# Gated linear attention with an MLP-mixer behind it, one core: u of batch 0 built transposed in PSUM, weight pieces of three chunks, another order

## The chip, the core and the metric

One core of one Trainium2 chip runs the whole program. The metric is the device time of one execution in microseconds; the time of a kernel is the median of its runs.

## The reference, cut to what matters

```python
# attention: q, k, v, alpha are (4 batches, 8 heads, 768 steps, 48)
for t in range(S):
    state = alpha[:, :, t, :, None] * state + einsum('bhd,bhe->bhde', k[:, :, t], v[:, :, t])
    y[:, :, t] = einsum('bhd,bhde->bhe', q[:, :, t], state)
# x is y with its heads side by side: (4, 768, 384)
# token and channel mixer, w_tok1 (768, 256), w_tok2 (256, 768), w_ch1 (384, 1536), w_ch2 (1536, 384)
h = maximum(x.T @ w_tok1, 0) @ w_tok2
u = x + h.T
out = u + maximum(u @ w_ch1, 0) @ w_ch2
```

Inputs and output are float32.

## The kernel before

The work of a batch is attention in three chunks of 256 time steps (chunks n = 0 to 11 over the four batches, `NB = 3`) and then a mixer. Every operation is written down once in `build` as `P.op(name, engines, ...)`, and two tables of numbers and names, `ORDER` and `BUFS`, say on which engine and in which place of that engine's program each stands, and which buffer it uses. A name in `ORDER` carries its engine as last letter: t is TensorE (PE), s ScalarE (ACT), v VectorE (DVE), g GpSimd (POOL), y the queue of SyncE (SP), which starts the loads, some stores and the transposing DMAs. Each engine takes its list strictly in that order and waits at an operation until what it reads is there.

Of a chunk n: `ld_at`, `ld_kt`, `ld_qt`, `ld_vt` load alpha, k, q and v (384 KB each). ACT takes the logarithm (`ln`), PE sums it over time (`cum`), ACT makes the decays `E` and `IE`, and `kk`, `qq` scale k and q (line 700). They are turned by PE (`trk`, `trq`, line 712, chunks 0 to 5) or by a transposing DMA (`dk`, `dq`, chunks 6 to 11), and `evk`, `evq`, `pq` copy them out. PE forms the masked scores (`G0`, `G1`; DVE masks them in line 770), the sums for the state (`K`), what comes from the state (`ia`, `ib`) and the outputs (`y0`, `y1`). The state runs on through `sa` (DVE, line 841) and `sm` (POOL or DVE, line 844): `sm1` of a chunk feeds the next. `vb`, `vs`, `ka`, `kb`, `kc` are casts and copies that bring v and k to other partitions. `P`, `k0a`, `q0r` are elementwise products. `x0`, `x1` evict the chunk's output as one of the six x tiles of a batch.

Of a batch b: `t1_b_m_kc` (line 878) multiplies with the first token weight, `ht` applies relu, `t2_b_i` (line 883) multiplies with the second one and gives the i-th 128 rows of h; `u_b_i` (DVE, line 887) adds x. The first channel product needs u transposed. For batch 0 (`UP = (0,)`) PE does that with 18 identity products of 128 columns (`up_0_p`, line 894) and three copies bring them from PSUM to `ut`; for batches 1 to 3 a transposing DMA on SP's queue does it (`ux_b_half`). `c1_b_mc_half` (line 902, three matmuls) and its relu `rt`, `c2_b_i_q4` (line 907, three matmuls), the sum `o` with u (DVE, line 911) and the store `st` end the batch. `f..` are fillers: PE multiplies zeros into an unused bank where it would else stand still.

The weights come as 16 pieces of 384 KB (`ldw_`), each cast to bf16 (`cw_`, line 746) by POOL, ACT or DVE. A piece of w_ch1 holds one chunk of 128 rows by 768 columns, so that each `c1` with mc below 6 needs pieces 0, 1 and 2, and the others need 3, 4 and 5:

```python
preds=(uts[0:2 + half] if b in UP else [uts[half]]) + [wl[("wc1", p)] for p in ((0, 1, 2) if mc < 6 else (3, 4, 5))]
```

Both pieces of w_tok2 (128 of its 256 rows each) are needed by every `t2`.

Of the kernel before, what the change touches and what calls it, by code (L numbers as in the profile page):

```python
# [56 lines left out]
def either(*ds):  # L57
    out = {}
    for d in ds:
        out.update(d)  # L60
    return out
# [40 lines left out]
UP = (0,)  # L102
# [18 lines left out]
def build(g):  # L121

    P = Plan()
# [6 lines left out]
    def fillers():  # L130
        for o in list(P.ops):
            nm = o.name
            if "PE" in o.eng and (nm[:4] in ("t1_0", "t2_0", "up_0") or nm.split("_")[-1][-1] in "0123" and nm[:2] not in ("t1", "t2", "up", "c1", "c2") and not nm.endswith("10") and not nm.endswith("11")):
# [182 lines left out]
    def mixer(b):  # L316
# [15 lines left out]
        us = []  # L332
        for i in range(NS):
            if i % 3 == 0:
                u = V("u")
            bank = V("one")
            o = P.op(f"t2_{b}_{i}", pe([384] * 2), m0 + (1900 + 330 * i) * sc, writes=[bank],
                     reads=[h for h, _ in hts], preds=[h for _, h in hts] + [wl[("wt2", p)] for p in range(2)],
                     emit=lambda e, i=i, bank=bank: g.tok2(bank, i, [h for h, _ in hts]))
            uo = P.op(f"u_{b}_{i}", dve(384), m0 + (1950 + 330 * i) * sc, writes=[u], reads=[bank, x[i][0]], preds=[o],  # L340
                      emit=lambda e, i=i, bank=bank, u=u: g.uadd(u, i, bank, x[i][0]))
            us.append((u, uo))
        ut = V("ut")
        uts = []
        if b in UP:
            for p in range(3):
                bank = V("one")
                o = P.op(f"up_{b}_{p}", pe([128] * 6), m0 + (3900 + 340 * p) * sc, writes=[bank],
                         reads=list(dict.fromkeys([us[2 * p][0], us[2 * p + 1][0]])),
                         preds=[us[2 * p][1], us[2 * p + 1][1]],  # L350
                         emit=lambda e, p=p, bank=bank: g.utr(bank, [us[2 * p][0], us[2 * p + 1][0]], p))
                uts.append(P.op(f"ut_{b}_{p}", either(dve(768, True), act(768)), m0 + (3950 + 340 * p) * sc, writes=[ut],
                                reads=[bank], preds=[o], emit=lambda e, p=p, bank=bank: g.utev(e, ut, bank, p)))
        else:
            for half in range(2):
                uts.append(P.op(f"ux_{b}_{half}", {"SP": (1240.0, 1240.0)}, m0 + (3900 + 500 * half) * sc, writes=[ut],
                                reads=[us[3 * half][0]], preds=[us[3 * half + i][1] for i in range(3)],
                                emit=lambda e, half=half: g.uxbar(ut, us[3 * half][0], half),
                                dma=("x", 1450.0, 1180.0, 480.0)))
# [13 lines left out]
        for i in range(NS):  # L373
            hold = 4000.0 if (i >= NS - 3 and b < B - 1) else 0.0
            cuts = [(0, HD // 2), (HD // 2, HD)] if (b, i) == LAST else [(0, HD)]
            for ci, (ca, cz) in enumerate(cuts):
# [33 lines left out]
ld_at1y ld_at0y ln1s ln0s f8_cumw1t f1_cumw1t cumw1t IE1s cumw0t IE0s ld_vt0y E0s vb0g vs0_0g vs1_0v ld_kt0y kk0v  # L410
f8_trk0t f1_trk0t trk0t E1s ld_qt0y qq0v ka0s kb0s kc0v f1_trq0t trq0t ld_kt1y kk1v K0t evq0s s0_0v ld_vt1y vb1s
f1_trk1t trk1t ld_at2y evk0v ln2s f2_G0_0t G0_0t ld_qt1y ka1g sa1_0v f4_cumw2t cumw2t mask0_0v vs0_1s kb1g kc1g vs1_1s
K1t sm1_0g qq1v sa0_1v sm0_1v G1_0t ld_kt2y IE2s E2s trq1t evq1s ib0t mask1_0v f3_y1_0t y1_0t y0_0t evk1v G0_1t sa1_1v
ld_qt2y x1_0s mask0_1v G1_1t ld_vt2y x0_0s vb2s kk2g trk2t kc2s ldw_wt10y qq2g cw_wt10s f2_ia1t ia1t mask1_1v evk2s
trq2t ld_at3y vs1_2g ldw_wt11y evq2v ib1t y1_1t y0_1t vs0_2g ldw_wt21y sm1_1g P3g K2t sa0_2v sm0_2g x0_1s t1_0_0_0t
f1_G0_2t G0_2t ldw_wt20y G1_2t cw_wt20g t1_0_1_0t mask0_2v x1_1s t1_0_1_1t ld_at4y ld_kt3y t1_0_1_2t lnP3s cum3t
cw_wt11s IE3s ia2t y0_2t x0_2s t1_0_0_1t t1_0_0_2t E3s t1_0_0_3t mask1_2v t1_0_1_3t ib2t y1_2t ldw_wc14y t1_0_1_4t
x1_2s t1_0_0_4t f1_t1_0_1_5t t1_0_1_5t ht_0_1v P4g cw_wt21s t1_0_0_5t ht_0_0s f3_t2_0_0t t2_0_0t t2_0_1t u_0_0v ln13s
r13s ldw_wc13y t2_0_2t u_0_1v t2_0_3t u_0_2v t2_0_5t lnP4s t2_0_4t u_0_3v u_0_5v u_0_4v up_0_0t cw_wc14s cw_wc13s
ldw_wc15y up_0_1t ld_qt3y k0a3g kk3g cum4t trk3t cw_wc15g ut_0_0v up_0_2t ut_0_2v ut_0_1s c1_0_11_0t c1_0_8_0t IE4s  # L420
c1_0_11_1t rt_0_8_0v rt_0_11_0v ldw_wc11y q0r3g qq3g c1_0_9_1t rt_0_9_1v ln14s kb3s c1_0_10_0t cw_wc11s c1_0_9_0t
rt_0_9_0v rt_0_11_1v E4s c1_0_7_0t c1_0_10_1t c1_0_7_1t ldw_wc10y r14s cw_wc10s rt_0_10_1v trq3t evk3s rt_0_7_0v
ldw_wc12y ld_vt3y cw_wc12g c1_0_2_0t c1_0_0_1t ka3g rt_0_7_1s c1_0_8_1t rt_0_10_0v vb3v vs1_3g vs0_3g rt_0_0_1v
rt_0_2_0v evq3s ld_at5y ld_qt4y c1_0_1_1t rt_0_8_1v c1_0_3_0t kc3s K3t P5g c1_0_4_1t rt_0_3_0s rt_0_1_1s q0r4g G0_3t
ld_kt4y qq4g s0_3v ln15s G1_3t sa1_3v c1_0_2_1t rt_0_2_1s mask0_3v lnP5s c1_0_1_0t c1_0_5_1t rt_0_5_1s rt_0_1_0s r15s
mask1_3v ldw_wc21y cw_wc21s k0a4g ldw_wc20y c1_0_6_1t rt_0_6_1v c1_0_4_0t kk4v ldw_wc22y c1_0_5_0t c1_0_0_0t cw_wc22s
rt_0_4_0v rt_0_0_0v cw_wc20g rt_0_4_1s c1_0_6_0t rt_0_6_0v c1_0_3_1t trq4t rt_0_3_1v cum5t trk4t ld_kt5y k0a5g
ldw_wc23y rt_0_5_0s c2_0_3_0t c2_0_5_0t evq4s kb4s evk4v ld_qt5y G1_4t mask1_4v G0_4t ld_vt4y c2_0_0_0t IE5s c2_0_0_1t
ka4g cw_wc23s c2_0_3_1t kc4s sm1_3g E5s mask0_4v ib3t y1_3t ldw_wc24y cw_wc24s c2_0_5_1t vb4g vs1_4s x1_3s ia4t
ldw_wc25y vs0_4g cw_wc25s ld_at6y y0_3t kk5v c2_0_3_2t y0_4t q0r5v trk5t evk5s qq5v K4t c2_0_0_2t sa0_4v c2_0_0_3t P6v  # L430
x0_3s ld_at7y sm0_4g o_0_0v trq5t x0_4s sa1_4v P7g evq5s lnP6s c2_0_5_2t c2_0_5_3t ld_vt5y vb5g c2_0_4_0t c2_0_4_1t
ld_kt7y kc5g G1_5t G0_5t lnP7s o_0_5v ib4t y1_4t vs1_5s mask1_5v t1_1_1_0t t1_1_1_1t sm1_4g x1_4s c2_0_4_2t c2_0_3_3t
vs0_5s ld_at8y t1_1_1_2t st_0_5s K5t mask0_5v sa0_5v sm0_5v cum6t t1_1_0_0t ld_kt6y k0a6g t1_1_0_1t ld_qt6y c2_0_2_0t
ln17s ld_qt7y ia5t y0_5t x0_5s IE6s kk6g ib5t y1_5t ln16s E6s t1_1_0_2t x1_5v t1_1_0_3t t1_1_1_3t cum7t E7s o_0_3v
t1_1_1_4t t1_1_1_5t r16s ld_kt8y q0r6g ld_vt6y dk6y P8g ht_1_1v lnP8s t1_1_0_4t t1_1_0_5t c2_0_2_1t c2_0_2_2t ln18s
ht_1_0v t2_1_1t u_1_1v t2_1_2t t2_1_0t t2_1_4t u_1_2v u_1_0v ux_1_0y c2_0_1_0t c2_0_1_1t vb6s IE7s qq6v r17s t2_1_3t
u_1_3v c2_0_2_3t ka6s kc6s t2_1_5t o_0_2v u_1_4v c2_0_1_2t st_0_0y st_0_3s cum8t k0a8g c2_0_1_3t u_1_5v q0r7v vs1_6v
dq6y c2_0_4_3t c1_1_8_0t rt_1_8_0v IE8s c1_1_11_0t vs0_6s c1_1_5_0t E8s c1_1_10_0t o_0_4v c1_1_4_0t k0a7g ux_1_1y
o_0_1v kb6g rt_1_4_0v pq6s K6t s0_6v sa1_6v c1_1_3_0t rt_1_3_0v c1_1_0_0t rt_1_5_0s ld_at9y rt_1_0_0v rt_1_11_0s
# [526 lines left out]
```

## Time and profile before

| | us |
|---|---|
| time, median of 3 runs | 163.17 (162.33 to 164.11) |
| span of the profiled execution, first to last instruction | 160.5 |
| PE busy | 154.6 (96%) |
| DVE, ACT, POOL busy | 114.9, 97.8, 80.8 |
| mean DMA rate | 218 GB/s |

The profiled execution has no time beside its span; the table's first row comes from other executions, which also count what lies before the first and behind the last instruction. Rows of the profile give start and duration in us from the span's start. "PE" rows are matmuls, whose duration (some 326 ns for 384 columns) runs through the pipeline, so that matmuls overlap: the pace is the time from one start to the next. "PEld" rows are the weight loads beside them.

### The profile page before, as it was taken

How to read it: one execution, taken by the hardware profiler on the slowest of the kernel's cores; microseconds unless marked ns; L12 is line 12 of the kernel's file. 1: busy time of each engine (PE TensorE's matmuls, PEld its weight loads, DVE VectorE, ACT ScalarE, POOL GpSimd, SP SyncE). 2: the span in 40 equal slices, each digit the busy share in tenths (PEclk: the TensorE clock that was granted, in tenths of full speed). 3: DMA queues.
4: the chain of work that ended last, by engine and by line, in shares of the span. 5: the costliest groups of instructions: out<-in, count | busy, mean ns of one | idle time of the engine just before them, and what ended most of it. 6: DMA issues, size and time to landing. Idle time of an engine off the chain costs nothing.

```text
span 160.5 us, 3971 instructions
## 1 busy us (share of the span) xinstructions
PE 154.6 (96%) x1563; PEld 97.1 (60%) x1563; DVE 114.9 (72%) x206; ACT 97.8 (61%) x179; POOL 80.8 (50%) x94
## 2 busy tenths in 40 slices
PE   7999989999999999999999999999999999999992
PEld 2545565766667676666667666566567665665661
DVE  6099994979889787989969758795886762464222
ACT  3789999998899955897563583269832203343000
POOL 5205897695973649389778852699523000000000
PEclk9999999999999999999999999999999999999999
DMA  4999999999999999999989999989701235111133
GB/s 122 320 324 317 317 374 311 339 333 306 316 347 324 275 278 272 210 228 319 241 202 298 239 315 204 217 196 134 196 21 62 87 79 169 49 49 53 49 129 116
DMA packets 76130, 35.05 MB, mean 218 GB/s; under 512 B 70352, under 2 KB 74320, under 8 KB 76112
## 3 DMA queue, kind: packets, MB, share of 16 engines
q1 hardware_dynamic: 73808, 31.76, 74.1%
q10 hardware_dynamic: 2304, 3.05, 5.3%
q8 instruction: 12, 0.20, 0.5%
q14 instruction: 6, 0.05, 0.1%
HBM read 25.17 MB, written 4.72 MB: 186 GB/s over the span
## 4 chain that ended last, share of the span: by engine, by line
PE 61%; DMA 12%; DVE 6%; ACT 6%; SPq 6%; POOL 4%; issue 3%; DVEq 0%; POOLq 0%
PE ps L907 22%; PE ps L902 21%; PE ps L643 11%; DMA in<-in_v_dram 6%; SPq L584 6%; DMA out_dram<-o 4%; PE ps L878 3%; PE ps L883 2%; DMA ut<-u 2%; DVE pkk L700 2%; DVE gtm L770 1%; PE ps L712 1%; DVE rt L875 1%; POOL vb L746 1%; POOL pkq L700 1%
## 5 line engine op out<-in xcount | busy, mean ns | idle before, releaser
L907 PE MATMUL ps<-wc,rt 128*128 128x384 bf16 (+1 forms) x300 | 52.4, 319 | 0.0
L902 PE MATMUL ps<-ut,wc 128*128 128x384 bf16 x288 | 50.3, 326 | 0.1
L902 PEld LDWEIGHTS <-wc 128*128 128x128 bf16 x288 | 27.1, 98 | 17.9 <-DMA ut<-u 0.6
L907 PEld LDWEIGHTS <-rt 128*128 128x128 bf16 x300 | 27.8, 98 | 16.0
L873 ACT ACTIVATE rt<-ps 128x384 bf16<-128x384 f32 x47 | 21.4, 492 | 23.6 <-PE ps L902 23.3
L875 DVE TENSOR_SCALAR rt<-ps 128x384 bf16<-128x384 f32 x49 | 25.6, 551 | 9.1 <-PE ps L902 8.9
L770 DVE TENSOR_TENSOR gtm<-ps,mk 128x1024 bf16<-128x1024 f32 x24 | 28.5, 1218 | 3.1 <-PE ps L643 2.8
L911 DVE TENSOR_TENSOR o<-ps,u 128x384 f32<-128x384 f32 (+1 forms) x25 | 13.2, 536 | 12.6 <-PE ps L907 10.1
L700 POOL TENSOR_TENSOR pkk<-in,IE 128x768 bf16<-128x768 f32 x8 | 14.5, 1817 | 3.3 <-DVE ss L844 2.3
L745 ACT CAST x<-ps 128x384 bf16<-128x384 f32 x20 | 9.2, 479 | 11.1 <-PE ps L643 9.5
L887 DVE TENSOR_TENSOR u<-ps,x 128x384 bf16<-128x384 f32 x24 | 12.0, 550 | 3.1 <-PE ps L883 2.5
L746 POOL CAST vb<-in 64x384 bf16<-64x384 f32 (+1 forms) x14 | 8.3, 594 | 10.4 <-DMA in<-in_v_dram 4.7
L692 POOL TENSOR_TENSOR in<-in,in 128x384 f32<-128x384 f32 x8 | 8.0, 1000 | 10.5 <-DVE u L887 3.8
L643 PE MATMUL ps<-rt 128*128 128x512 bf16 (+1 forms) x29 | 12.1, 515 | 1.1 <-DVE rt L541 1.1
L745 ACT CAST vb<-in 64x384 bf16<-64x384 f32 (+1 forms) x18 | 11.4, 634 | 0.8 <-DMA in<-in_v_dram 0.3
L700 POOL TENSOR_TENSOR pkq<-in,E 128x768 bf16<-128x768 f32 x6 | 10.9, 1818 | 0.6 <-DMA tpk<-pkq 0.3
L878 PE MATMUL ps<-x,wt 128*128 128x384 bf16 x48 | 11.0, 325 | 0.0
L844 POOL TENSOR_TENSOR ss<-tmp,E 128x384 bf16<-128x384 f32 x10 | 8.3, 833 | 4.2 <-DVE in L628 3.9
L841 DVE TENSOR_TENSOR tmp<-ps,ss 128x384 f32<-128x384 f32 x16 | 8.8, 552 | 1.8 <-PE ps L643 0.6
L883 PE MATMUL ps<-ht,wt 128*128 128x384 bf16 x48 | 9.1, 326 | 0.0
L643 PE MATMUL ps<-vb,gtm 128*128 128x48 bf16 x192 | 8.2, 183 | 0.2 <-DVE gtm L770 0.2
L643 PE MATMUL ps<-tpq,tpk 48*64 48x128 bf16 (+1 forms) x288 | 7.9, 218 | 0.4 <-POOL tpq L746 0.3
(94 smaller groups left out, 207.6 us busy)
## 6 DMA issues: line engine op xcount, KB each, us to landing
in<-in_alpha_dram SPq DMA_DIRECT2D x12, 384.0 KB, 5.1
in<-in_v_dram SPq DMA_DIRECT2D x12, 384.0 KB, 5.6
in<-in_k_dram SPq DMA_DIRECT2D x12, 384.0 KB, 5.2
in<-in_q_dram SPq DMA_DIRECT2D x12, 384.0 KB, 5.5
in<-in_moe_w_ch_dram SPq DMA_DIRECT2D x12, 384.0 KB, 5.9
out_dram<-o ACTq DMA_DIRECT2D x15, 192.0 KB, 1.8
in<-in_moe_w_tok_dram SPq DMA_DIRECT2D x4, 384.0 KB, 6.0
out_dram<-o SPq DMA_DIRECT2D x8, 192.0 KB, 2.2
```

The lines of the kernel that those rows point to most:

```text
L643: return self.pe.matmul(out, lhsT=lhsT, rhs=rhs, start=start, stop=stop, skip_group_check=True)
L700: self.shared(self.eng[e].tensor_tensor(self.t(dst)[:, :, h0:h1, 0:D], self.t(src)[:, h0:h1].rearrange("p h s d -> p s h d"), bass.AP(tens ...
L745: return self.act.copy(d, s)
L770: self.nc.vector.tensor_tensor(self.t(gtm)[:, hf, :, :], self.pair(gp).rearrange("p a (j t) -> p (a j) t", t=128), bass.AP(tensor=m.tensor ...
L873: self.act.activation(d, s, AF.Relu)
L875: self.nc.vector.tensor_scalar_max(d, s, 0.0)
L878: self.pe.matmul(self.bank(bank)[:, 0:HD], lhsT=self.wt1[:, kc, m * 128 : m * 128 + 128], rhs=self.t(x), start=(kc == 0), stop=(kc == NS - 1))
L883: self.pe.matmul(self.bank(bank)[:, 0:HD], lhsT=self.wt2[:, kc, i * 128 : i * 128 + 128], rhs=self.t(hts[kc]), start=(kc == 0), stop=(kc = ...
L887: self.nc.vector.tensor_tensor(self.t(u)[:, i % 3], self.bank(bank)[:, 0:HD], self.t(x), ALU.add)
L902: self.pe.matmul(self.bank(bank)[:, 0:HD], lhsT=self.wc1[:, kc, mc * 128 : mc * 128 + 128], rhs=self.t(ut)[:, 3 * half : 3 * half + 3, kc, ...
L907: self.pe.matmul(self.bank(bank)[:, 0 : cz - ca], lhsT=self.t(rts[mc][0])[:, i * 128 : i * 128 + 128], rhs=self.wc2[:, mc, ca:cz], start=( ...
L911: self.nc.vector.tensor_tensor(self.t(o)[:, ca:cz], self.bank(bank)[:, 0 : cz - ca], self.t(u)[:, i % 3, ca:cz], ALU.add)
```

## The change

Batch 0 no longer makes u and turns it. For each half (three row blocks of 128) and each j (a block of 128 of the 384 channels), `xa_0_half_j` puts the three x blocks transposed into a PSUM bank by products with the identity, `tt_0_half_j` adds the second token product in transposed form into the same bank, and one copy `ut_0_half_j` (ACT or DVE) brings the sum to `ut`. u in its plain form is never made for batch 0: the residual at the end enters the PSUM bank of `c2_0_i_0` by three further identity products (`resid`), and `o_0_i` becomes a plain copy by ACT or DVE.

The pieces of w_ch1 and w_tok2 are cut by columns: piece p of w_ch1 holds 256 columns of all three chunks, so that `c1` with mc needs only piece mc // 2, and piece p of w_tok2 the 384 columns of half p. Their DMA rows are 1024 and 1536 bytes instead of 3072.

`ORDER` and `BUFS` are new throughout: other loads first, other places and engines for most operations.

```diff
-UP = (0,)
+UP = ()
+UDIR = (0,)
...
+        if b in UDIR:
+            ut, us, uts = V("ut"), [], []
+            for half in range(2):
+                evs = []
+                if half in (0, 1):
+                    for j in range(NM):
+                        bank = V("one")
+                        tx = x[3 * half : 3 * half + 3]
+                        xa = P.op(f"xa_{b}_{half}_{j}", pe([128] * 3), m0 + (1700 + 900 * half + 60 * j) * sc, writes=[bank],
+                                  reads=[v for v, _ in tx], preds=[o for _, o in tx],
+                                  emit=lambda e, bank=bank, tx=tx, j=j: g.xadd(bank, [v for v, _ in tx], j))
+                        o = P.op(f"tt_{b}_{half}_{j}", pe([384] * 2), m0 + (1900 + 900 * half + 330 * j) * sc, writes=[bank],
+                                 reads=[h for h, _ in hts], preds=[h for _, h in hts] + [xa, wl[("wt2", half)]],
+                                 emit=lambda e, bank=bank, half=half, j=j: g.tok2t(bank, half, j, [h for h, _ in hts]))
+                        evs.append(P.op(f"ut_{b}_{half}_{j}", either(act(384), dve(384)), m0 + (1950 + 900 * half + 330 * j) * sc,
+                                        writes=[ut], reads=[bank], preds=[o],
+                                        emit=lambda e, bank=bank, half=half, j=j: g.utev3(e, ut, bank, half, j)))
...
-                         reads=[ut], preds=(uts[0:2 + half] if b in UP else [uts[half]]) + [wl[("wc1", p)] for p in ((0, 1, 2) if mc < 6 else (3, 4, 5))],
+                         reads=[ut], preds=(uts[half] if b in UDIR else uts[0:2 + half] if b in UP else [uts[half]]) + [wl[("wc1", mc // 2)]],
...
-                                emit=lambda e, i=i, q4=q4, bank=bank, ca=ca, cz=cz: g.ch2(bank, i, q4, rts, ca, cz))
+                                emit=lambda e, i=i, q4=q4, bank=bank, ca=ca, cz=cz, ri=ri: (g.ch2(bank, i, q4, rts, ca, cz), g.resid(bank, ut, i) if ri else None))
...
 ORDER = """
-ld_at1y ld_at0y ln1s ln0s f8_cumw1t f1_cumw1t cumw1t IE1s cumw0t IE0s ld_vt0y E0s vb0g vs0_0g vs1_0v ld_kt0y kk0v
+ld_kt1y ld_at0y ln0s f12_cumw0t f2_cumw0t cumw0t ld_at1y ln1s cumw1t ld_kt0y IE0s E0s kk0v f2_trk0t trk0t kb0v IE1s
...
         elif nm == "wc1":
-            c, h = piece % 3, piece // 3
-            self.gated(dma(t, self.w[2][128 * c : 128 * c + 128, 768 * h : 768 * h + 768]), op)
+            w = self.w[2].rearrange("(c p) m -> p c m", p=128)
+            self.gated(dma(t.rearrange("p (c m) -> p c m", c=3), w[:, :, 256 * piece : 256 * piece + 256]), op)
...
+    def xadd(self, bank, xs, j):
+        for i, x in enumerate(xs):
+            self.mm(self.bank(bank)[:, i * 128 : i * 128 + 128], self.t(x)[:, j * 128 : j * 128 + 128], self.idn, i == 0, False)
+
+    def tok2t(self, bank, half, j, hts):
+        for kc in range(NDT):
+            self.mm(self.bank(bank)[:, 0:HD], self.t(hts[kc])[:, j * 128 : j * 128 + 128],
+                    self.wt2[:, half, kc, :], False, kc == NDT - 1)
...
+    def resid(self, bank, ut, i):
+        for j in range(NM):
+            self.mm(self.bank(bank)[:, j * 128 : j * 128 + 128], self.t(ut)[:, i, j, :], self.idn, False, False)
```

Three places of the new order. The first is POOL's program at the start, behind its memsets. `pkk` and `pkq` are the scaled k and q of a chunk (`kk`, `qq`), `ss` the states (`sm`), `vb` casts and half copies of v, `wt` a cast token weight, `L628` and `L654` the product `P`. Before:

```order
L746 CAST vb_98<-in_76 128x768
L746 CAST vb_98<-in_76 64x384
L746 COPY kt_97<-pkk_95 64x8x48 x2
L746 COPY pkk_95<-pkk_95 64x8x48
L844 TENSOR_TENSOR ss_112<-tmp_109,E_88 128x384
L700 TENSOR_TENSOR pkk_96<-in_65,IE_91 128x16x48
L700 TENSOR_TENSOR pkq_93<-in_78,E_87 128x16x48
L746 CAST vb_100<-in_68 64x384 x2
L844 TENSOR_TENSOR ss_114<-tmp_109,E_89 128x384
L628 TENSOR_TENSOR in_79<-in_79 128x8x48
L844 TENSOR_TENSOR ss_111<-tmp_109,E_87 128x384
```

and of the change:

```order
L726 TENSOR_TENSOR pkk_96<-in_71,IE_90 128x16x48
L772 CAST vb_99<-in_72 64x384
L870 TENSOR_TENSOR ss_112<-tmp_109,E_87 128x384
L772 CAST wt_156<-in_76 128x768
L870 TENSOR_TENSOR ss_113<-tmp_110,E_88 128x384
L654 TENSOR_TENSOR in_75<-in_75 128x8x48
L870 TENSOR_TENSOR ss_114<-tmp_109,E_88 128x384
L772 CAST wt_156<-in_78 128x768
L870 TENSOR_TENSOR ss_111<-tmp_110,E_89 128x384
```

The first state product (`ss_112`, sm1_0) stood ahead of the scaled k of chunk 2 (`pkk_96`); now it stands behind it, all four state products of the first batch are POOL's, and casts of both token weight pieces stand between them.

The second is SP's program at the start (row 1 is its first DMA), before:

```order
1 L584 DMA in_75<-in_alpha_dram 128x8x96
2 L584 DMA in_72<-in_alpha_dram 128x8x96
3 L584 DMA in_76<-in_v_dram 128x8x96
4 L584 DMA in_64<-in_k_dram 128x8x96
9 L584 DMA in_76<-in_q_dram 128x8x96
10 L584 DMA in_65<-in_k_dram 128x8x96
11 L584 DMA in_78<-in_q_dram 128x8x96
12 L584 DMA in_68<-in_v_dram 128x8x96
```

and of the change:

```order
1 L608 DMA in_69<-in_k_dram 128x8x96
2 L608 DMA in_64<-in_alpha_dram 128x8x96
3 L608 DMA in_65<-in_alpha_dram 128x8x96
4 L608 DMA in_66<-in_k_dram 128x8x96
8 L608 DMA in_70<-in_v_dram 128x8x96
10 L608 DMA in_72<-in_v_dram 128x8x96
11 L608 DMA in_71<-in_k_dram 128x8x96
12 L608 DMA in_74<-in_v_dram 128x8x96
```

The k of chunk 2 was the tenth load and is the eleventh; the v of chunk 0 was the third and is the eighth; the v of chunk 2 is the twelfth in both.

The third is SP's program where it turns u of batch 2, before:

```order
L584 DMA in_64<-in_k_dram 128x8x96
L624 DMA out_dram<-o_155 128x384
L624 DMA out_dram<-o_153 128x384
L729 DMA_TRANSPOSE ut_131<-u_128 128x9x128
L729 DMA_TRANSPOSE ut_131<-u_127 128x9x128
```

and of the change:

```order
L608 DMA in_80<-in_k_dram 128x8x96
L608 DMA in_82<-in_v_dram 128x8x96
L755 DMA_TRANSPOSE ut_131<-u_129 128x9x128
L755 DMA_TRANSPOSE ut_131<-u_130 128x9x128
L650 DMA out_dram<-o_154 128x384
```

The two stores that stood ahead of the two turns are gone from there; one store follows them.

More of the change, by code (lines that the diff above doesn't have):

```diff
@@ L331, in mixer @@
             hts.append((ht, ho))
[L332 to L342, printed above, removed]
@@ L882, in tok2 @@
         for kc in range(NDT):
-            self.pe.matmul(self.bank(bank)[:, 0:HD], lhsT=self.wt2[:, kc, i * 128 : i * 128 + 128], rhs=self.t(hts[kc]),
+            self.pe.matmul(self.bank(bank)[:, 0:HD], lhsT=self.wt2[:, i // 3, kc, i % 3 * 128 : i % 3 * 128 + 128], rhs=self.t(hts[kc]),
                            start=(kc == 0), stop=(kc == NDT - 1))
```

204 lines of the change are left out of this document (112 added, 92 removed), and 22 rows, old and new, of the table BUFS.

## The prediction

> **What bounds the kernel now.** I read the page first, then the busy time in two stretches, then the chain of waits from its end, then PE's groups behind 31.7 us, and last the timeline of the start.
>
> ```profile
> span 160.5 us, 3971 instructions
> PE 154.6 (96%) x1563; PEld 97.1 (60%) x1563; DVE 114.9 (72%) x206; ACT 97.8 (61%) x179; POOL 80.8 (50%) x94
> PE   7999989999999999999999999999999999999992
> PEclk9999999999999999999999999999999999999999
> 0.00:32.00 32.00, 29.69 (x319) 16.79 (x320) 23.51 (x53) 26.63 (x41) 18.41 (x31) 1.00 1.02 303
> 32.00:158.00 126.00, 124.95 (x1246) 80.27 (x1244) 91.35 (x154) 71.22 (x139) 62.37 (x64) 1.00 0.75 199
> ...
> 133.97 10.72 PE ps L902 x66
> 147.62 9.79 PE ps L907 x72
> 157.44 0.36 DVE o L911
> ```
>
> PE is busy in every slice, and the last 24 us of the chain are nothing but PE. 66 matmuls of 384 columns in 10.72 us are a pace of 0.1624 us. With that pace the groups of PE behind 31.7 us can be turned into work without waits:
>
> ```profile
> L907 PE MATMUL ps<-wc,rt 128*128 128x384 bf16 x276 | 50.7, 326 | 0.0
> L902 PE MATMUL ps<-ut,wc 128*128 128x384 bf16 x288 | 50.3, 326 | 0.1
> L878 PE MATMUL ps<-x,wt 128*128 128x384 bf16 x36 | 8.3, 325 | 0.0
> L883 PE MATMUL ps<-ht,wt 128*128 128x384 bf16 x36 | 6.8, 326 | 0.0
> L643 PE MATMUL ps<-vb,gtm 128*128 128x48 bf16 x144 | 6.4, 183 | 0.0
> L643 PE MATMUL ps<-ss,tpq 128*128 128x96 bf16 x60 | 5.0, 206 | 0.0
> L643 PE MATMUL ps<-tpq,tpk 48*64 48x128 bf16 x192 | 3.8, 219 | 0.3 <-POOL tpq L746 0.3
> ```
>
> The first four are 636 matmuls, 103.3 us. The small shapes overlap in their busy figures, so I price them by start-to-start distances in the timeline: all the rest together (the three rows below, the sums for the state, turns, cumulative sums, the 24 half matmuls) comes to some 20.2 us. That is 123.5 us of work between 31.8 and 157.2, a stretch of 125.5 us: **PE waits there only about 2.0 us in all**. So the kernel has two parts: a start of 31.8 us that ends with the first c1, where PE waits and is filled up with zeros, and a saturated part in which time is the sum of PE's work. A change can win at most those 2.0 us in the second part; anything more must come from the start.
>
> **The change part by part.** All of it is reckoned against the span of 160.5 us. The timed median is 163.17, 2.7 us above it, and I add the difference of spans to the median.
>
> *The start up to the last t1 of batch 0.* This is where the order matters.
>
> ```profile
> 11.88 1.14 SPq L584 DMA_DIRECT2D in<-in_q_dram  x1
> 13.07 1.14 SPq L584 DMA_DIRECT2D in<-in_v_dram  x1
> 16.84 1.82 POOL L700 TENSOR_TENSOR pkk<-in,IE 128x768 bf16<-128x768 f32 x1 [2.30 <-DVE ss L844]
> 19.34 0.83 ACT L745 CAST vb<-in 128x768 bf16<-128x768 f32 x1
> 23.17 1.22 DVE L770 TENSOR_TENSOR gtm<-ps,mk 128x1024 bf16<-128x1024 f32 x1
> L841 DVE TENSOR_TENSOR tmp<-ps,ss 128x384 f32<-128x384 f32 x16 | 8.8, 552 | 1.8 <-PE ps L643 0.6 <-POOL ss L844 0.5
> L844 POOL TENSOR_TENSOR ss<-tmp,E 128x384 bf16<-128x384 f32 x10 | 8.3, 833 | 4.2 <-DVE in L628 3.9
> L628 POOL TENSOR_TENSOR in<-in 128x384 f32<-128x384 f32 x8 | 8.0, 999 | 0.4 <-DMA in<-in_alpha_dram 0.3
> L746 POOL CAST wt<-in 128x768 bf16<-128x768 f32 x1 | 0.8, 823 | 0.6 <-DMA in<-in_moe_w_tok_dram 0.6
> L746 POOL CAST vb<-in 64x384 bf16<-64x384 f32 x10 | 5.0, 502 | 5.7 <-DVE ss L844 3.7 <-DVE vb L746 1.6
> ```
>
> The twelfth load (issued 13.07) was cast at 19.34, 6.3 us later. The eleventh was issued at 11.88, so with the same delay it is there at 18.15. In the change this is the k of chunk 2, and POOL's list behind it is a chain: scaled k 1.82 (to 19.97), half of v 0.50 (20.5), sm1_0 0.83 (21.3), a cast 0.82 (22.1), sm0_1 0.83 (22.95), P3 1.0 (23.9), sm1_1 0.83 (24.75), a cast 0.82 (25.6), sm0_2 0.83 (26.45). DVE's four masks (1.22 each, issued every 1.14) and the sa's (0.55) run beside it and are ready when POOL needs them: by my walk through its list the last mask of chunk 2 ends at 26.5. Then PE does ib2 and y1_2 (0.6), DVE evicts x1_2 (0.55, to 27.6), and the last t1's end at 28.0. Before they ended at 26.85 (two matmuls from 26.52, below). **+1.15 us.** Ends: if the eleventh load comes 1 us sooner, the walk is held by the v of chunk 2 and ACT behind it instead and gains only 0.2; if something in my walk overlaps that I have put in a row, at best all of it goes, 0; if that load comes 1.5 us later, the whole chain shifts with it. So 0 to +2.7.
>
> *From t1 to the first c1.*
>
> ```profile
> 26.52 0.48 PE L878 MATMUL ps<-x,wt 128*128 128x384 bf16 x2
> 26.94 0.86 PE L643 MATMUL ps<-rt 128*64 128x384 f32 x2
> 27.73 2.28 PE L883 MATMUL ps<-ht,wt 128*128 128x384 bf16 x12
> 29.85 0.83 PE L894 MATMUL ps<-idn,u 128*128 128x128 bf16 x12
> 30.81 0.61 PE L712 MATMUL ps<-idn,pkk 128*128 128x128 bf16 x8
> 31.25 0.50 PE L894 MATMUL ps<-idn,u 128*128 128x128 bf16 x6
> 31.76 1.46 PE L902 MATMUL ps<-ut,wc 128*128 128x384 bf16 x8
> ```
>
> From 26.85 to 31.76 are 4.9 us. The work in them: 12 token matmuls 1.95, 18 turns at (0.83 - 0.22) / 11 = 0.056 us, 1.0, a cumulative sum 0.33 and the turns of k 0.45: 3.7. The other 1.2 us are the filler behind the relu of ht (0.86) and waits for u and its copies. The change does the same 12 token matmuls and 18 identity products, and needs no u in between. The relu wait is covered by six identity products and the cumulative sum of chunk 4 (0.34 + 0.33), and the turns of q and k of chunk 3 lie between the tt's; the second half's w_tok2 and the first w_ch1 piece are the 20th and 21st load and, at the 1.2 us from load to load seen above, come near 28 to 29, ahead of their use at 30.8 and 32. I put 0.1 us of wait: 3.8 us for what took 4.9. **-1.1 us**; if the cover is gone, it is the whole relu wait again, -0.3.
>
> *Identity products for the residual.* 18 more of 0.056 us, in the saturated part, where nothing hides them: **+1.0 us** (the same row; 0.8 to 1.1).
>
> *Waits in the saturated part.* The two places where PE visibly waits on the transposing DMA:
>
> ```profile
> PEld L902 <- DMA ut<-u: 0.6, 2, 0.5
> 93.33 5.63 DMA out_dram<-o
> 98.95 3.12 DMA ut<-u
> ```
>
> The turns of u for batch 2 queued behind a store and landed as PE came to need them. In the new order they stand ahead of the store. By the pace above some 5 us of PE work lie between the last token matmul of a half of that batch and its first c1, against a DMA of 3.1 us and adds of 0.55 on DVE, so that the turns have a microsecond to spare where they start at once; several turns of k and q are likewise further ahead of their scores. I take half the waits away, 2.0 to 0.9: **-1.1 us**. Ends: -2.0 (none left) to +2.0 (as many again; every one of some 300 evictions has a new place and a bank that the next product wants 1.0 to 1.5 us later, and no row of before shows those).
>
> *Nothing.* DVE loses six adds of 0.55, ACT and DVE gain copies of about 0.5; both have idle time in the saturated part (91 and 71 of 126 us busy), so this is covered by PE, and without cover it would be 3 us of DVE saved. Shorter DMA rows cost nothing as far as the page shows:
>
> ```profile
> in<-in_moe_w_ch_dram SPq DMA_DIRECT2D x12, 384.0 KB, 5.9
> in<-in_moe_w_tok_dram SPq DMA_DIRECT2D x4, 384.0 KB, 6.0
> ```
>
> All twelve of the first have rows of 3072 bytes, half of the second 1024, and they land in 5.9 and 6.0 us. At the end the last operation is again a sum of half a row block, 0.36 us, and one store.
>
> Sum: 1.15 - 1.1 + 1.0 - 1.1 = -0.05, a span of 160.5 and a time of **163.1 us**: no change. Its own range, with the load and the waits each off by a microsecond, is 161.8 to 164.5.
>
> **The rivals.** *Faster:* the start costs nothing (the loads come sooner than the walk has them) and the waits shrink to 0.4: 0 - 1.1 + 1.0 - 1.6 = -1.7, 161.4 us. For it: the turns no longer stand behind stores, and the work of the start is the same. Against: POOL's chain above is long and has no gap.
>
> *Slower:* POOL's chain in the start. It decides from the landing of k of chunk 2 on: each microsecond behind 18.15 goes one for one into the last t1, since POOL stands at the scaled k and everything behind it waits, and PE has nothing but t1 products left. Landing at 19.9 or later makes +1.75, 164.9 us. For it: this load was the tenth and is the eleventh, and before POOL had nothing else behind it in the state's chain. Against: a start in which loads come late would have been late before, too, by its twelfth load.
>
> *The change moves waits without removing any:* the u adds that fall away were hidden, the start is as long as before, and only the residual's products remain, +1.0, 164.2 us.
>
> *The clock.* Two rows with the same seven fillers show two paces of PE:
>
> ```profile
> 1.06 4.21 PE L643 MATMUL ps<-rt 128*64 128x384 f32 x7 [1.06 <-DVE rt L541]
> 7.34 2.26 PE L643 MATMUL ps<-rt 128*64 128x384 f32 x7
> ```
>
> The first seven take 1.9 times as long, although the granted clock reads 9 in each slice. If PE stood still long enough in the new start to fall back to the slow pace for as long as those 4.2 us, the work in them would take 2 us more: 165.1 us. In the walk PE's longest pause is about 1.1 us (before the turns of k of chunk 2), so I give it little. The Trainium skill (TensorE: Matmul & The Clock Gate, Part 1: The HAM clock gate) says that the array drops to half its clock after an idle window of about 3.4 us; by that rule a pause of 1.1 us would do nothing, and the two paces above agree with its factor of two.
>
> **How the numbers follow.** Forecast 0.40 and "only the residual" 0.08 lie within 1%: 0.48. Faster by over 1%, which is about what a measurement of this kernel can tell from no change (its three runs lie 1.1% apart): 0.27, the first rival. Slower by over 1%: POOL's chain 0.21 and the clock 0.04, 0.25. The range 160.6 to 165.6 goes to the ends of start and waits taken one at a time (-2.0 and +2.0 on the waits, +1.5 on the load) and somewhat beyond, since two new tables of the whole order hold more than I can walk through.
>
> **What would show it.** In the profile after: the last t1 of batch 0 ends near 28.0 us and the first c1 starts near 32.3 (the start is right); POOL goes from the scaled k of chunk 2 to sm0_2 without a gap; 18 identity products from x and 18 from ut in rows of their own at 0.056 us; PE's waits behind 32 us sum to about 1 us, and none of them names the turns of u; the span is within a microsecond of 160.5. A first c1 before 31 or after 33.5, or waits of over 2.5 us behind it, would make the prediction wrong.

## The result, and the profile after

The changed kernel takes 167.01 us (166.12 to 167.79), the kernel before 163.64 beside it: a ratio of 1.0256, 95% interval 1.0214 to 1.0299. Run again later beside other kernels (e9 below) it is at 1.0193 (1.0149 to 1.0236). Ratios leave out executions that ran clearly slower than their like (the largest is one of e13 at 199.94 us), the medians in us do not, so that a ratio need not follow from two medians. So the change made the kernel about 2 to 2.5% slower, 3 to 4 us, where no change was forecast.

Lines of the page of the changed kernel:

```profile
span 164.4 us, 4017 instructions
PE 155.2 (94%) x1580; PEld 97.9 (60%) x1580; DVE 115.7 (70%) x204; ACT 97.8 (60%) x186; POOL 72.4 (44%) x86
in<-in_moe_w_ch_dram SPq DMA_DIRECT2D x12, 384.0 KB, 6.1
out_dram<-o ACTq DMA_DIRECT2D x13, 192.0 KB, 3.7
```

Its busy time behind the first c1 (the columns are the stretch, its length, the busy time of PE, PEld, DVE, ACT and POOL with their instructions, PE's granted clock, and the share and rate in GB/s of the DMA):

```profile
33.20:161.20 128.00, 126.29 (x1257) 80.70 (x1256) 90.83 (x152) 72.00 (x145) 55.82 (x58) 1.00 0.77 197
```

PE has hardly more busy time than before (155.2 against 154.6 us), but the span is 3.9 us longer. Where it went is seen by the start of the first c1 product and of the last matmul in the timelines: 31.76 and 157.16 before, 33.24 and 160.83 after. The start is 1.5 us longer. The stretch behind it is 2.2 us longer (127.59 against 125.40), of which 1.0 is the residual's products; the turns of q of chunk 3, 0.45, have left it for the start. Priced as in the prediction, PE's waits there are therefore some 3.7 us (2.0 + 2.2 - 1.0 + 0.45) where they were 2.0.

The chain that ended last shows the longest of these waits. Columns are start, length, and the engine with the line that ran, or what was waited for:

```profile
94.00 0.38 PE ps L669 x12
94.38 0.02 issue
94.40 0.28 ACT x L771
94.68 4.57 DMA out_dram<-o
99.26 0.03 issue
...
99.35 0.06 DVE o L953
...
99.82 0.55 DVE in L654
100.37 1.08 DVE u L913 x3
```

In the kernel before the chain ran here over a store and then the turns of u (the rows at 93.33 and 98.95 in the prediction). Now the store is followed by DVE: its sum `o`, a product of alpha, and the additions of u. The timeline of DVE, ACT's queue and PE says what this is (square brackets hold the idle time of the engine just before a row, and what ended it):

```profile
86.18 1.02 DVE L953 TENSOR_TENSOR o<-ps,u 128x384 f32<-128x384 f32 x2
94.68 0.34 ACTq L650 DMA_DIRECT2D out_dram<-o  x1
95.06 0.45 ACTq L650 DMA_DIRECT2D out_dram<-o  x1
99.35 0.56 DVE L953 TENSOR_TENSOR o<-ps,u 128x384 f32<-128x384 f32 x1 [4.53 <-DMA out_dram<-o]
99.96 0.49 PE L909 MATMUL ps<-ht,wt 128*128 128x384 bf16 x2 [0.65 <-DVE o L953]
100.89 0.49 PE L909 MATMUL ps<-ht,wt 128*128 128x384 bf16 x2 [0.45 <-DVE u L913]
```

DVE makes `o_1_1` and `o_1_2` by 87.2. Their stores stand on ACT's list behind a dozen other things and are issued at 94.7 and 95.1, 7.5 us later and more; the first, that of `o_1_2`, lands 4.57 us after its issue. There are three `o` buffers, and `BUFS` gives `o_1_5` that of `o_1_2`. So DVE stands 4.53 us at `o_1_5`, everything behind it on DVE waits, the u additions of batch 2 among it, and `t2_2_2` and `t2_2_0` find their PSUM banks not yet emptied. By name, in the list of waits (total, times, longest), of the kernel before:

```profile
DVE o L911 <- DMA out_dram<-o: 2.5, 3, 1.6
```

and of the changed kernel, where the other of the two, 2.0 us, stands before the last sum of the program and stays in e13:

```profile
DVE o L953 <- DMA out_dram<-o: 6.5, 2, 4.5
```

The store itself is not slower than it was. The page of the kernel before has a median of 1.8 us for ACT's stores, but the one that it issued there in the same stretch, at 90.91, took longer than the 4.57 us of the changed kernel's (the second row, of the view for 90 to 97 us alone):

```profile
out_dram<-o ACTq DMA_DIRECT2D x15, 192.0 KB, 1.8
out_dram<-o ACTq DMA_DIRECT2D x1, 192.0 KB, 5.6
```

What the change made new is the place of the store, 7.5 us behind its sum where that one was 3.3 behind its own, and a next user of the buffer that comes 4.5 us before it lands.

### The profile page after: what moved, and what is told of

It is laid out like the page before. It is cut to its first block, busy times and chain, and to the rows that moved or that the text cites. A ratio compares the mean times of both kernels' runs of the same rounds, so it can differ in the third digit from the quotient of the medians.

```text
span 164.4 us, 4017 instructions
## 1 busy us (share of the span) xinstructions
PE 155.2 (94%) x1580; PEld 97.9 (60%) x1580; DVE 115.7 (70%) x204; ACT 97.8 (60%) x186; POOL 72.4 (44%) x86
## 4 chain that ended last, share of the span: by engine, by line
PE 55%; DMA 17%; POOL 9%; SPq 8%; DVE 4%; issue 3%; ACT 1%; POOLq 0%; DVEq 0%
PE ps L949 20%; PE ps L944 19%; PE ps L669 8%; SPq L608 6%; DMA in<-in_moe_w_tok_dram 4%; DMA in<-in_alpha_dram 4%; DMA in<-in_q_dram 3%; PE ps L904 3%; DMA tpk<-pkk 3%; DMA out_dram<-o 3%; PE ps L909 2%; POOL pkk L726 2%; POOL pkq L726 2%; PE ps L738 2%; DVE u L913 1%
## 5 line engine op out<-in xcount | busy, mean ns | idle before, releaser
L953 DVE TENSOR_TENSOR o<-ps,u 128x384 f32<-128x384 f32 (+1 forms) x19 | 9.9, 533 | 14.1 <-PE ps L949 7.3
L771 ACT CAST vb<-in 64x384 bf16<-64x384 f32 (+1 forms) x22 | 13.5, 612 | 5.1 <-POOL vb L772 4.2
L726 POOL TENSOR_TENSOR pkk<-in,IE 128x768 bf16<-128x768 f32 x7 | 12.7, 1816 | 6.4 <-DVE in L718 4.9
L870 POOL TENSOR_TENSOR ss<-tmp,E 128x384 bf16<-128x384 f32 x13 | 10.9, 836 | 6.0 <-DVE tmp L867 6.0
L669 PE MATMUL ps<-rt 128*64 128x384 f32 (+1 forms) x28 | 10.8, 499 | 1.1 <-DVE rt L565 1.1
L771 ACT CAST x<-ps 128x384 bf16<-128x384 f32 x16 | 7.6, 478 | 6.9 <-PE ps L669 6.6
L726 POOL TENSOR_TENSOR pkq<-in,E 128x768 bf16<-128x768 f32 x5 | 9.1, 1817 | 5.6 <-ACT E L702 4.5
L913 DVE TENSOR_TENSOR u<-ps,x 128x384 bf16<-128x384 f32 x18 | 8.8, 549 | 2.2 <-PE ps L909 2.0
L772 POOL CAST wc<-in 128x768 bf16<-128x768 f32 x8 | 6.8, 866 | 7.6 <-DVE pkk L726 5.5
L669 PEld LDWEIGHTS <-tpk 48*64 48x64 bf16 (+1 forms) x288 | 6.0, 102 | 4.7 <-issue 3.0
```

The source lines that it names most:

```text
L669: return self.pe.matmul(out, lhsT=lhsT, rhs=rhs, start=start, stop=stop, skip_group_check=True)
L726: self.shared(self.eng[e].tensor_tensor(self.t(dst)[:, :, h0:h1, 0:D], self.t(src)[:, h0:h1].rearrange("p h s d -> p s h d"), bass.AP(tens ...
L771: return self.act.copy(d, s)
L772: return self.shared(self.eng[e].tensor_copy(d, s))
L870: self.shared(self.eng[e].tensor_tensor(self.st(self.t(s)), self.st(self.t(t)), self.amul(E, hf, wide), ALU.mult))
L913: self.nc.vector.tensor_tensor(self.t(u)[:, i % 3], self.bank(bank)[:, 0:HD], self.t(x), ALU.add)
```

## Experiments

All ratios are to the kernel before on the same chip. "First c1" is the start of that product in the profiled execution. The profiled executions of e4 and e7 lie 1.9 and 0.7 us above their medians; of these two I read only the place in question.

| run | what | us | ratio (95%) | first c1 |
|---|---|---|---|---|
| e1 | old order, new pieces alone | 163.42 | 1.0028 (1.0000 to 1.0055) | 31.93 |
| e2 | old order, whole structure | 166.18 | 1.0178 (1.0130 to 1.0227) | 32.33 |
| e7 | e2, two channel blocks exchanged | 164.55 | 1.0067 (1.0031 to 1.0104) | 31.31 |
| e9 | the change again | 165.72 | 1.0193 (1.0149 to 1.0236) | 31.87 |
| e3 | change, k of chunk 2 in its own buffer | 164.56 | 1.0105 (1.0079 to 1.0132) | 31.98 |
| e4 | change, two stores earlier | 164.05 | 1.0067 (1.0035 to 1.0099) | 33.07 |
| e8 | change, fourth output buffer | 163.45 | 1.0026 (0.9991 to 1.0061) | 31.64 |
| e13 | e8 again | 163.34 | 1.0012 (0.9979 to 1.0045) | 31.81 |
| e12 | e8 and e3 | 162.95 | 0.9992 (0.9965 to 1.0018) | 32.28 |
| e5 | e3 and e4 | 162.48 | 0.9970 (0.9938 to 1.0001) | 32.02 |
| e10 | e3, e4 and e8 | 162.71 | 1.0032 (1.0008 to 1.0055) | 32.01 |
| e6 | change without the residual products | 164.46 | 1.0073 (1.0035 to 1.0112) | 32.04 |
| e14 | e12 without them | 162.18 | 0.9948 (0.9924 to 0.9972) | 32.04 |
| e11 | e5 with u made in the old way | 170.67 | 1.0425 (1.0367 to 1.0483) | 37.54 |

My theory was that the loss lies in the new order, at two buffers: the output buffer above, and the input buffer of k of chunk 2. The rival was that the structure itself (pieces, identity products, bank use) costs more than I had priced.

**The output buffer: e4, e8, e13.** e4 moves the two stores up on ACT, e8 gives `o_1_5` the space of an input buffer that is idle then.

```diff
 # e4, ORDER
-... IE9s st_1_2s kk9g ... y0_8t st_1_1s x0_8s ...
+... rt_1_6_1s st_1_1s rt_1_11_1s st_1_2s y1_6t ...
 # e8
+self.T["o"].append(self.T["in"][17].rearrange("p h s d -> p (h s d)")[:, 0:HD])
-# o_1_5 in output buffer 1
+# o_1_5 in output buffer 3
```

> The changed kernel, with the stores of rows 1 and 2 of batch 1 issued by ACT some 7 us earlier, behind two relu evictions of the same stretch, at the same cost on ACT; nothing else moves. Theory (the output buffer of row 5 was held by a store that landed at 99.26, which stalled DVE 4.53 us and PE 1.4 us): the stall is gone, 1.0 to 1.5 us faster than the changed kernel's 167.0, so 165.5 to 166.0. Rival (the next late thing stands right behind, the u additions and the loads of chunks 9 and 10): less than 0.5 us of it is seen.

> The changed kernel, with the output of row 5 of batch 1 put into the space of an idle input buffer, so that it waits for no store; the stores stay where they are. Theory (the output buffer was the cause): the stall of 1.4 us is gone, as with the early stores of e4, ratio to before 1.007 to 1.016. Rival (the gain of e4 came from the place of the stores, on ACT or in the stream of transfers): 1.020 or more.

> The kernel of e8 again, beside e12: a ratio to before of 1.000 to 1.006 as there, with a spread of 2 us.

Both cures work by different means, and the stores of e8 are issued where they stood in ACT's list, so it is the buffer and not the place of the stores as such. Both gained more than expected: e4 came to 164.05 us where 165.5 to 166.0 was expected, e8 to 1.0026 where 1.007 to 1.016 was. In e13 the chain of the same stretch reads:

```profile
92.91 0.18 PE ps L905
93.09 0.76 PE ps L670 x24
93.85 1.47 PE ps L905 x9
95.31 0.97 PE ps L950 x6
96.29 1.95 PE ps L910 x12
98.24 2.92 PE ps L950 x18
```

It is PE from end to end, and in the timeline the row of `o_1_5` has no wait:

```profile
93.00 0.55 DVE L954 TENSOR_TENSOR in<-ps,u 128x384 f32<-128x384 f32 x1
```

PE's busy time in the same 3.41 us of e9, the change run again, and of e13:

```profile
95.85:99.26 3.41, 1.96 (x12) 0.97 (x10) 1.53 (x4) 0.00 (x0) 0.42 (x1) 1.00 0.76 243
95.85:99.26 3.41, 3.41 (x23) 2.06 (x22) 3.16 (x7) 1.68 (x5) 1.21 (x2) 1.00 0.76 245
```

From the first c1 to the last matmul e13 takes 125.50 us where the change took 127.59 and, in e9, 127.24: 1.7 to 2.1 us less. In the times the fourth buffer is worth more, 1.7 to 2.4% or 2.7 to 4.0 us. Of e9 the profiled execution was the fastest of those measured (164.4 against a median of 165.72), so its profile shows less than the usual loss. What the longer executions lose beyond 2 us was not profiled; it goes when the buffer is free, but where in them it lies is open. One part may be PE's clock: its granted mean is 0.99 in one of the first four executions of the change, in two of the six of e9 and in four of the twelve of e6, which all have the stall, and at least 0.996 in all those of e5, e8, e10 and e12, where the stall is gone. What such a mean can come from is seen in e11 below; that the stall brings it is not shown, since no such execution of the change was profiled.

**The change again: e9.**

> The changed kernel itself, run again beside the others. Theory (its first four runs were high: single cures cannot bring three times the wait that they remove): a ratio to before of 1.014 to 1.020, with which the cures are worth 0.5 to 1.0% each and their sum is that of e5. Rival (the first measurement holds, and each cure also frees transfers elsewhere): 1.023 or more.

It came out at the theory's upper end. Its profile has the same stall, and nothing of the long start of the first one: the first c1 is at 31.87.

```profile
DVE o L953 <- DMA out_dram<-o: 6.9, 2, 4.9
PE ps L909 <- DVE o L953: 1.0, 1, 1.0
PE ps L909 <- DVE u L913: 0.4, 1, 0.4
```

**The input buffer of k of chunk 2: e3, e12.** That load is the eleventh. It reuses the buffer of the seventh, q of chunk 1, and DVE frees that at 13.49, when it has scaled q. The start of the changed kernel, SP's queue, POOL and PE:

```profile
11.11 1.33 SPq L608 DMA_DIRECT2D in<-in_v_dram  x1
13.51 0.37 SPq L608 DMA_DIRECT2D in<-in_k_dram  x1
18.78 1.82 POOL L726 TENSOR_TENSOR pkk<-in,IE 128x768 bf16<-128x768 f32 x1 [1.14 <-DMA in<-in_k_dram]
26.31 0.83 POOL L870 TENSOR_TENSOR ss<-tmp,E 128x384 bf16<-128x384 f32 x1
33.24 0.66 PE L944 MATMUL ps<-ut,wc 128*128 128x384 bf16 x3
```

SP's queue stands 1.07 us between 12.44 and 13.51, with every later load behind it. e3 gives the load a buffer of its own:

```diff
-# input buffers: ld_kt2 7, ld_qt3 15
+# input buffers: ld_kt2 15, ld_qt3 7
```

> The changed kernel, with the load of k of chunk 2 put into an input buffer that nothing uses before it (and q of chunk 3 into the one it leaves); no instruction moves. Theory (the eleventh load waits 1.07 us for a buffer, and every later load and POOL's chain to the last t1 inherit that): its issue at 12.4 to 12.5 in place of 13.51, the last t1 and the first c1 0.9 to 1.2 us earlier, the whole 0.8 to 1.3 us faster than the changed kernel's 167.0, so 165.7 to 166.2. Rival (POOL's own work sets the last t1, or the stream of loads is full anyway): less than 0.3 us of it is seen.

The time is 0.9% below that of e9, more than expected. The issue comes at 11.52, and the first c1 1.26 us sooner than in the first profile. But so it does in e9, which has the old buffer. Set side by side on one chip:

> The changed kernel with the fourth output buffer and with k of chunk 2 in its own input buffer; no instruction moves. Theory (the buffer wait costs only where the seventh load lands a microsecond late, as in the first profile of the changed kernel, 12.43 against 11.5): the median 0.3 to 0.9% below e13 beside it, with a narrower spread. Rival (the buffer is off the path, as the same first c1 at 31.9 to 32.0 with and without it says): within 0.2% of e13.

e12 is 0.2% below e13 and the intervals overlap, as the rival had it; of the theory only the narrower spread is there (161.99 to 163.42 against 162.15 to 165.38, without the 199.94). In e12 the load goes out at 11.62 and POOL gets it no sooner:

```profile
11.62 1.15 SPq L609 DMA_DIRECT2D in<-in_k_dram  x1
18.00 1.82 POOL L727 TENSOR_TENSOR pkk<-in,IE 128x768 bf16<-128x768 f32 x1 [1.22 <-DMA in<-in_k_dram]
```

In e13, issued at 12.52, that POOL row starts at 17.79. In these two the load comes when the stream of loads brings it. In e3 and e5, with the same buffer, it landed sooner, at 16.3 and 16.4, and the first c1 came at 31.98 and 32.02 all the same. The long start of the first profile goes with late early loads: the seventh landed at 12.43 there, at 11.4 to 11.5 in all but one of the other profiles of this order (12.76 in e4, whose first c1 is also late, at 33.07). That the shared buffer makes such executions worse is possible, since DVE frees it only after that load; e3 against e9 (0.9%, on different chips) would fit. It is not shown.

**Both: e5, e10.**

> The changed kernel with both cures: k of chunk 2 in its own input buffer, and the two stores of batch 1 issued early. Theory (two separate waits at two places): their measured gains of 1.5% and 1.9% add up, 161.4 to 162.2 us where the kernel before takes 163.0, so 0.5 to 1.0% faster than before. Rival (both shifted the same later transfers against the same work, and one gain hides the other): no better than the early stores alone, 163.5 to 164.3.

> The changed kernel with k of chunk 2 in its own input buffer, the two early stores, and the fourth output buffer as well. Theory (after e5 no output buffer is waited for any more): the same as e5, ratio to before 0.994 to 1.000. Rival (stores still hold buffers in runs with late transfers): 0.990 or less.

e5 is level with the kernel before, perhaps 0.3% faster, short of the 0.5 to 1.0% expected; e10, which adds to e5 only a buffer that nothing in e5 waits for, is 0.3% slower. They ran on different chips, and I take half a per cent between chips for more than these runs can settle. With the output buffer free, the changed kernel is as fast as the one before, and no version that computes the whole result beats that one clearly.

**The residual: e6, e14.** The edit leaves the three identity products per row block out of `c2_0_i_0`:

```diff
-emit=lambda e, ...: (g.ch2(bank, i, q4, rts, ca, cz), g.resid(bank, ut, i) if ri else None)
+emit=lambda e, ...: g.ch2(bank, i, q4, rts, ca, cz)
```

> The changed kernel with the 18 identity products of the residual left out (the rows of batch 0 then lack u), at 0.056 each on PE; all else stands. Theory (saturated PE, so PE work is worth its time): 0.8 to 1.1 us faster than the changed kernel, a ratio to before of 1.018 to 1.021. Rival (the later waits are for transfers that come at their own time): 0.3 us or less, 1.024 or more.

> The kernel of e12 with the 18 identity products of the residual left out (the rows of batch 0 lack u). Theory (PE is saturated there): 0.8 to 1.1 us faster than e12. Rival (transfers set the later pace): 0.4 us or less.

e6 is 1.2% below e9, twice the work that went and outside what theory and rival had; it still has the stall, and a long start or none by chance, so it priced nothing. e14 beside e12 gives 0.8 us (0.44%). The work that went is 18 products at 0.056 us, 1.0; the rows in the changed kernel's profile are

```profile
L669 PE MATMUL ps<-idn,ut 128*128 128x128 bf16 x18 | 2.0, 219 | 0.0
L669 PE MATMUL ps<-idn,x 128*128 128x128 bf16 x18 | 1.8, 219 | 0.0
```

with no wait ahead of either. The theory holds, at the low end.

**The structure without the new order: e1, e2, e7.** e1 takes the new pieces with the old order and old u; e2 also makes u of batch 0 transposed, each `tt` where a `t2` stood, each `ut` copy where a u addition stood; e7 exchanges channel blocks 9 and 11 in e2.

```diff
 # e1
-UP = ()
-UDIR = (0,)
+UP = (0,)
+UDIR = ()
 # e2, ORDER of the kernel before
-f3_t2_0_0t t2_0_0t t2_0_1t u_0_0v ... up_0_0t ... up_0_1t ... ut_0_0v up_0_2t ut_0_2v ut_0_1s
+xa_0_0_0t xa_0_0_1t xa_0_0_2t tt_0_0_0t tt_0_0_1t ut_0_0_0v ... tt_0_1_1t ut_0_1_0s ut_0_1_2v ut_0_1_1v
 # e7, on top of e2
-c1_0_11_0t c1_0_8_0t ... c1_0_11_1t ... c1_0_9_1t ...
+c1_0_9_0t c1_0_8_0t ... c1_0_9_1t ... c1_0_11_1t ...
```

> The three-chunk pieces of wc1 and the two-chunk pieces of wt2 under the old order; u of batch 0 made, turned and added as before. Theory (the loss of the changed kernel lies in its new order): the same as before, within 0.5 us of the 163.6 us that it took beside the changed kernel. Rival (the pieces themselves slow the stream of loads: six pieces, each 0.2 us later, all ahead of the first c1 products): 0.6 to 1.2 us slower than before.

> The whole structural change (transposed u of batch 0, identity products for x and for the residual, new pieces) under the old order: each turn of the old u step is replaced where it stood, nothing else moves. Theory (the loss lies in the new order): the first c1 product comes 0.7 to 1.1 us earlier than at 31.76, 1.0 us of residual products is added later, so 163.6 us plus or minus 0.8. Rival (the structure costs more than its products: bank turns, x held longer, weight pieces): 165.5 us or more.

The pieces cost nothing that can be measured. The structure cost 1.5% more, against the theory. PE and POOL in e2, where PE has done its turns of k by 31.0:

```profile
30.42 0.61 PE L738 MATMUL ps<-idn,pkk 128*128 128x128 bf16 x8
31.41 0.87 POOL L772 CAST wc<-in 128x768 bf16<-128x768 f32 x1 [1.55 <-DMA in<-in_moe_w_ch_dram]
32.33 0.99 PE L944 MATMUL ps<-ut,wc 128*128 128x384 bf16 x5 [1.31 <-POOL wc L772]
```

u is there earlier, but `c1_0_11_0` now waits for a weight: the piece that it needs lands at 31.35, and POOL casts it to 32.28. Behind the first c1 e2's profile is 2.8 us longer than e1's (129.20 against 126.36), 1.0 of it residual. Of the other 1.8 us I only know where PE stands still: 0.91 us at 109.33 for POOL's copy `tpq`, 0.58 at 94.97 for an x tile and 0.55 at 84.75 for a half of k, none of which e1 has; why the structure brings them is open.

> The structure under the old order (e2), with channel blocks 9 and 11 of the first mixer's channel step exchanged in the order, so that its first three products need only the weight piece that is cast at 30.6 and not the one that is cast at 32.28. Theory (the cast of the last piece, behind the product of k of chunk 3 on POOL, held the first c1, not the turns of u): first c1 at 30.7 to 31.1 in place of 32.33, and 1.0 to 1.4 us faster than e2, ratio to before 1.009 to 1.012. Rival (the next product, or the loads behind, take it back): ratio 1.015 or more.

With the products first whose piece is there, the wait is gone and the first c1 stands right behind the turns of k:

```profile
30.87 0.61 PE L738 MATMUL ps<-idn,pkk 128*128 128x128 bf16 x8
31.31 1.95 PE L944 MATMUL ps<-ut,wc 128*128 128x384 bf16 x11
```

31.31 is 0.2 us outside what was expected, and the time fell by 1.1%, 1.8 us, somewhat more than expected. Against e1 the structure now gains 0.6 us at the first c1, pays 1.0 for the residual, and is 0.4% slower, 0.6 us: about their difference, though the two ran on different chips and that is less than I allow between chips.

**The old u in the new order: e11.** By hand, in e5: `t2` and u additions where `tt` and `ut` stood, `up` and its copies ahead of the first c1. `o_0_2`, `o_0_4` and `o_0_5`, plain copies on ACT in e5, become sums on DVE again.

```diff
-tt_0_1_2t ... ut_0_1_2s ... tt_0_1_1t ... ut_0_0_2v ... c1_0_0_1t
+t2_0_5t t2_0_3t u_0_5v ... t2_0_4t u_0_3v u_0_4v ln14s qq3v trq3t evq3s up_0_2t ... up_0_0t kk3v trk3t up_0_1t ut_0_0s ut_0_1v ... c1_0_0_1t
```

> The kernel of e5 (the new order with both cures) with u of batch 0 made, turned and added in the old way, placed by hand where the transposed u stood. Theory (the transposed u buys what its residual products cost, 1.1 us before the first c1 against 1.0 us after it): within 0.6 us of e5, ratio to before 0.993 to 1.001. Rival A (the structure is what is worth having under this order, since DVE is full there): 1 us or more slower than e5, 1.004 or more. Rival B (the residual products are a loss): 0.6 us or more faster than e5, 0.993 or less.

It does not answer its question. My placing left PE without work for 1.8 us while DVE made u and scaled q, and then PE ran at half its clock. Busy time by stretch (columns as above), cut where the granted clock changes, and PE's rows on both sides of the pause:

```profile
27.75:31.16 3.41, 1.40 (x12) 0.73 (x11) 2.83 (x6) 1.46 (x4) 0.00 (x0) 1.00 1.08 337
31.16:34.57 3.41, 3.41 (x24) 2.37 (x22) 1.96 (x5) 1.96 (x2) 0.00 (x0) 0.50 1.13 335
34.57:37.98 3.41, 1.66 (x21) 1.10 (x19) 2.36 (x4) 1.31 (x2) 2.13 (x3) 1.00 0.77 253
37.98:41.40 3.42, 3.42 (x26) 1.83 (x25) 1.34 (x3) 1.90 (x4) 3.28 (x5) 0.50 0.04 8
```

```profile
27.98 1.14 PE L909 MATMUL ps<-ht,wt 128*128 128x384 bf16 x6 [0.21 <-DVE ht L901]
30.92 0.85 PE L738 MATMUL ps<-idn,pkq 128*128 128x128 bf16 x8 [1.80 <-DVE pkq L726]
32.20 2.12 PE L909 MATMUL ps<-ht,wt 128*128 128x384 bf16 x6
```

The clock is the smaller part of the loss. The profiled execution has a granted mean of 0.98, which its two stretches at 0.50 make; two of the six executions had 1.00 and took 168.42 and 168.66 us, one had 0.99 and took 170.31, three had 0.98 and took 171.03 to 171.45. Even those at 1.00 are 5.7 us or more above e10 (162.71 on the same chip), so most of the loss is my placing. What the transposed u is worth against a well placed old u under the new order remains open; e7 against e1, under the old order and on different chips, is the nearest comparison.

## Why the prediction was wrong

*The step that failed is the waits in the saturated part.* I took 2.0 to 0.9, -1.1 us; they went to 3.7 and, in e9, 3.3, over the 2.5 that I had named as the sign of being wrong. I had looked at the turns of u for batch 2, and those did come off the path: no wait of PE names them any more, as said under "what would show it". A store took their place, at nearly the same spot. The row was in my own fence: "93.33 5.63 DMA out_dram<-o" says that a store there takes over 5 us to land, and I read it only as what delays the turns behind it on the queue, not as what keeps an output buffer from its next user. The two tables show the rest without a run: the stores of `o_1_1` and `o_1_2` late on ACT's list, and `o_1_5` in the second one's buffer. My upper end for the waits, +2.0, covered the size, but I tied it to PSUM banks, named no place for it, and let the middle stand at -1.1. With the buffer free the waits are 1.2 (e12) and 1.6 (e13), not 0.9; that much of the step was optimistic in any case. What I put under *Nothing* has the same fault: I called DVE covered because it is idle for part of the saturated stretch, but its order is strict, and idle time elsewhere does not help an engine that stands 4.53 us at one place with PE's next bank behind it. These waits are 2.4 to 2.8 us above the forecast; of the 3 to 4 us in the times the rest lies in the late start of some executions and in what was not profiled.

*The start* was right in e9 and e13, and 0.9 us too short for the first profile. Last t1 forecast to end at 28.0: 28.9 in the first profile, 27.8 in e9, 27.7 in e13. The load of k of chunk 2, forecast for 18.15, landed at 18.6, 17.7 and 17.6. From t1's end to the first c1 I had 4.3 us with the turns of q and k; they took 4.4, 4.1 and 4.1. POOL's chain from the scaled k to sm0_2 took 8.4 us in the first profile (18.78 to 27.14) where I had 8.3.

*The residual* was right at +1.0 (e14: 0.8). *The pieces* were right at nothing (e1); the landing time of 6.1 against 5.9 us is within what other profiles of the same shape show (5.6 to 6.3).

*The rivals.* "POOL's chain in the start" named a slower result by another mechanism. It fits the start of the first profile, where the load came 0.5 us later than forecast and the last t1 0.9, but e9 still loses 1.9% without it, and e12 says that an earlier load changes little. The clock was full in both profiles of the changed kernel, but not in all of its executions: a mean of 0.99 in three of the ten says that this rival may have a part in the loss, which no run here prices. "Nothing is gained, only the residual is paid" comes closest to e7, under the old order.

*The sum* as forecast, 163.1, is that of the change without its one stall: 162.95 in e12, 163.34 in e13. That it fits so well is in part luck: in e13 the first c1 comes 0.5 us sooner than forecast and the waits behind it are 0.7 us more.

## What to carry to other kernels

A buffer belongs to its last reader, and of an output buffer that is a store: count the time from the add to the store's place on its issuing engine, and from there to its landing, before the next user of the buffer; an in-order engine that waits there stops all that stands behind it. When an earlier result is meant to bring work forward, look at what else that work reads: in e2 it was a weight cast, and exchanging two blocks of the order paid more than the change of structure. And profile the same kernel twice before a cure is credited with the difference.

## What the runs showed of the hardware

I had not expected the clock to fall in e11. In its profile the granted clock is 0.50 from 31.16 to 34.57 us and again from 37.98 to 41.40, each time for 3.41 us; six token matmuls take 2.12 us in the first of these stretches and 1.14 ahead of the pause. In the 3.41 us ahead of each fall PE is busy for only 1.40 and 1.66 us (the first and the third row of e11's fence), and its longest single pauses there are 1.80 and 1.01 us. The Trainium skill (TensorE: Matmul & The Clock Gate, Part 1: The HAM clock gate) has the gate fall after an idle window of about 3.4 us, and its table has two states, half and full clock. The two levels and the length agree with 0.50, 1.00 and 3.41 us here; but PE did not stand still for the whole of such a stretch in this profile, so the argument in my prediction that a pause of 1.1 us does nothing by that rule is weaker than I took it. In e2 PE paused 1.31 us ahead of the first c1 and the clock stayed full; a stretch of the same length around that pause has PE busy for 2.10 us:

```profile
29.51:32.92 3.41, 2.10 (x25) 1.48 (x24) 1.05 (x2) 3.18 (x6) 1.45 (x3) 1.00 1.06 339
```

So the falls followed shares of 0.41 and 0.49, and 0.62 brought none. Where the limit lies between them no run here shows, and the two executions of e11 at a mean of 1.00 say that the order of the program alone does not decide it.

A store takes long to land among loads, under either order: 192 KB issued on ACT's queue at 94.68 and 95.06 us took 4.6 and 5.6 us in the changed kernel, at 86.57 and 87.03 in e5 4.5 and 4.6, and at 90.91 in the kernel before 5.6. The median of 1.8 us on the page of the kernel before comes from others: its four stores on that queue between 113 and 127 us, where the load stream has all but ended (a mean of 90 GB/s, against 295 between 90 and 97), took 1.8 to 2.9.
